# Two fused expert layers behind a causal convolution: some convolutions summed by adding transfers, blocks 0 and 1 interleaved by eight

## The chip, the cores and the metric

The kernel runs on one core of a Trainium2 chip, as one launch. The metric is device time in microseconds. Three runs of the kernel before gave 1137.07, 1137.29 and 1139.7 us; their median, 1137.29 us, is the time to which the change is compared. The engines are named as in the profile: PE multiplies matrices, PEld is its weight load, DVE is VectorE, ACT is ScalarE, POOL is GpSimd, SP only issues transfers.

## The reference, cut to what matters

A causal convolution over 7 tokens, with weights per head made by a softmax, then two layers of "multiply, activate, multiply":

```
w   = softmax(weight)                      # 8 heads x 7 taps; 24 channels share a head
out = sum over k of w[k] * x[t - 6 + k]    # 2 x 4096 tokens, 192 channels
h   = out @ moe_w_in                       # 192 -> 2048
g   = h where h >= 1, 0 where h <= -1, (h + 1)^2 / 4 between
x2  = g @ moe_w_out                        # 2048 -> 192
h2  = x2 @ moe2_w_in
y   = (h2 * sigmoid(1.702 * h2)) @ moe2_w_out
```

Everything is float32 and has to come out with nearly float32's precision.

## The kernel before

**Tiling.** The 8192 tokens are 16 blocks of 512. Channels lie on partitions, tokens along the row. A layer's 2048 hidden channels are 16 groups of 128, numbered f = 0 to 15. One layer of one block is a phase, and one group of one phase is a unit. The 192 channels are two parts: part a is the first 128, part b the last 64; the b parts of two blocks (0 and 1, 2 and 3, and so on) share one tile of 128 partitions.

**Precision.** Each float32 operand is split in two halves of a shorter format, a high one by a copy on ACT (L73 for activations, L127 for weights) and the rest by a subtraction on DVE (L74, and L131 and L132 for weights), and products of halves are added in PSUM.

**A unit.** `gemm1(u)` makes the hidden values of unit u in one of four PSUM banks (5 matmuls, L250). `act_a(u)` activates them: for layer 1 an activation, a square on ACT (L272, L273) and a max-min on DVE (L274). `act_b(u)` splits the result (`ghi` on ACT, `glo` on DVE). `gemm2(u)` adds its product into the block's two output banks (5 matmuls, L315), LAG = 4 steps after `gemm1(u)`. For the first 32 units a step is `gemm1(step)`, `act_a(step)`, `act_b(step - 1)`, `gemm2(step - 4)`, in the lines L493 to L501. From unit 32 on (WHOLE) units go in pairs, with half-size matmuls that run two at a time (`both`, L361).

**Weights.** Weights arrive as 64-bit words and are converted on chip, once for each layer and f, in four pieces (`weight_ops`): `begin` (a Prelu on ACT, L117, tile `wa`, and a shift on DVE, L118, tile `wd`), `join` (DVE, L122), `high_part` (ACT, L127) and `low_part` (DVE, L131 and L132). `gemm1` of a unit needs both parts of its f. Raw words have three buffers, filled by transfers that SP issues.

**Order.** All engines run the program in the order in which the code issues it; no scheduler moves it. `plan` is a table from step to operations, filled by `at(step, op)`; `beside(step)` issues that step's operations. Units 0 to 31 are layer 1 of blocks 0 and 1, interleaved by CH = 4 (`in_turn`, L216): four units of block 0, four of block 1, and so on. Then follow 16 units of block 2, layer 2 of blocks 0 and 1, and layers 1 and 2 of the other blocks.

**Convolutions.** Block 0 and 1's b part and block 1's a part are done on PE, seven float32 matmuls against diagonal matrices (`conv_on_pe`, banks `cb_ps` and `ca_ps`, L170); block 1's diagonals are made by POOL (L167). Block 0's a part, and all of the later blocks, are done on DVE, one multiply and six multiply-adds for a tile (`conv_taps`, L152 and L153). `conv_at(j)` places those of blocks 2j and 2j + 1: for blocks 2 and 3, part a of block 2 in steps 10 to 17, part b of both in steps 18 to 25. `put_a` and `put_b` split the sums into the tiles `xah`, `xal`, `xb`, `xc`, which `gemm1` reads.

Of the kernel before, what the change touches and what calls it, by code (L numbers as in the profile page):

```python
# [8 lines left out]
F32 = mybir.dt.float32  # L9
# [3 lines left out]
ALU = mybir.AluOpType  # L13
# [7 lines left out]
def kernel(  # L21
# [44 lines left out]
    def bank(n, name):  # L66
        return ps.tile([P, T], F32, tag=f"bank{n}", name=name)
# [33 lines left out]
    def weight_ops(n, f, s):  # L101

        low, high = s[:, :, 0], s[:, :, 1]
        w = wt[n][:, f, :]  # L110
# [37 lines left out]
    def conv_taps(part, t, c):  # L148
        def tap(k):
            w, x = taps[:, part, k : k + 1], t[:, k : k + T]  # L150
            if k == 0:
                return lambda: nc.vector.tensor_scalar_mul(c, x, w)  # L152
            return lambda: nc.vector.scalar_tensor_tensor(c, x, w, c, op0=ALU.mult, op1=ALU.add)  # L153

        return [tap(k) for k in range(K)]

    def warm_up():

        w = bank(7, "warm")
        for _ in range(9):  # L160
            nc.tensor.matmul(w[:, 0:P], ident, ident, start=True, stop=True)  # L161

    def conv_on_pe(part, t, c, ident, eng_mul):

        d = o_p.tile([P, K, P], F32, tag="o", name="diag")
        for k in range(K):
            eng_mul(d[:, k], ident, taps[:, part, k : k + 1])  # L167

        def tap(k):
            return lambda: nc.tensor.matmul(c, d[:, k], t[:, k : k + T], start=k == 0, stop=k == K - 1)  # L170

# [9 lines left out]
    def put_b(i, c):  # L181

        b, halved = i % B, phases.index((1, i)) * NF >= WHOLE
        t = x1[i][2 + (b if halved else 0)]
        hi, lo = (t[0:DB], t[DB:P]) if b == 0 else (t[DB:P], t[0:DB])
        split(c[b * DB : (b + 1) * DB], hi, lo)
        if halved:
            swap_halves(x1[i][3 - b], t)

    def conv_ops(j):  # L190

        ta, tb = xt[0, B * j], xt[1, j]
        ca = cv_p.tile([P, T], F32, tag="cva", name="cva")
        cb = cv_p.tile([P, T], F32, tag="cvb", name="cvb", bufs=1)
        x1[B * j] = new_xs()
        ops = conv_taps(0, ta, ca) + [lambda: put_a(B * j, ca)]
        ops += conv_taps(1, tb, cb) + [lambda: put_b(B * j, cb)]
        st = {}

        def begin():  # L200
            st["c"] = cv_p.tile([P, T], F32, tag="cva", name="cva")
            x1[B * j + 1] = new_xs()
            st["ops"] = conv_taps(0, xt[0, B * j + 1], st["c"])
            put_b(B * j + 1, cb)
# [8 lines left out]
        phases += [(1, i), (2, i - 1)]  # L213
    phases += [(2, NBLK - 1)]

    def in_turn(*ps):  # L216
        return [(p, c + f) for c in range(0, NF, CH) for p in ps for f in range(CH)]

    units = in_turn(0, 1) + in_turn(2) + in_turn(3, 4)
    units += [(p, f) for p in range(5, len(phases)) for f in range(NF)]  # L220
    unit_at = {u: k for k, u in enumerate(units)}

# [181 lines left out]
    def at(step, op):  # L404
        plan.setdefault(max(step, 0), []).append(op)
# [14 lines left out]
    def fetch_x(*which):  # L420
        for part, i in which:
            xt[part, i] = x_load(part, i)

    def conv_at(j):
        first, second = (unit_at[phases.index((1, B * j + k)), 0] for k in range(B))
        ops = []
        at(first - 30, lambda: fetch_x((0, B * j), (1, j), (0, B * j + 1)))
        at(first - 22, lambda: ops.extend(conv_ops(j)))
        for k in range(2 * (K + 1)):
            at(first - 22 + k, lambda: ops.pop(0)())  # L430
        for k in range(K + 2):
            at(second - 16 + k, lambda: ops.pop(0)())

    with tc.manual_schedule():
        nc.sync.dma_start(taps, taps_in)
        fetch_x((0, 0), (1, 0))
        fetch_w(1, 0)
        fetch_w(1, 1)
        fetch_x((0, 1))
        fetch_w(1, 2)  # L440

        make_identity(nc, ident)
        warm_up()
        softmax_taps()

        nc.scalar.activation(const.tile([P, 1], F32, name="table"), ident[:, 0:1], AF.Gelu_apprx_sigmoid)
        for i in range(B):
            x1[i] = new_xs()
        ca = cv_p.tile([P, T], F32, tag="cva", name="cva")
        cb_ps, ca_ps = bank(3, "cb_ps"), bank(2, "ca_ps")  # L450
        a0 = conv_taps(0, xt[0, 0], ca)
        b_ops = conv_on_pe(1, xt[1, 0], cb_ps, ident, nc.scalar.mul)
        a1 = conv_on_pe(0, xt[0, 1], ca_ps, ident, nc.gpsimd.tensor_scalar_mul)
        for op in b_ops:
            op()

        ws = [weight_ops(1, f, raw.pop((1, f))) for f in range(CH - 1)]
        order = a0[0:3] + ws[0][0:1] + a0[3:5] + ws[0][1:3] + a0[5:7] + ws[0][3:4] + ws[1][0:1]
        order += [lambda: put_a(0, ca)] + ws[1][1:2] + [lambda: put_b(0, cb_ps)] + ws[1][2:] + ws[2]
        for op in order:  # L460
            op()
        fetch_w(1, 3)
        for k, op in enumerate(weights_at(1, 3)):
            at(k // 2, op)
        for k, op in enumerate(a1):
            at((k + 2) // 3, op)
        at(1, lambda: put_b(1, cb_ps))
        at(2, lambda: put_a(1, ca_ps))

        def convert_at(n, f, steps):  # L470
            at(steps[0] - 3, lambda: fetch_w(n, f))
            for step, op in zip(steps, weights_at(n, f)):
                at(step, op)

        for f in range(CH, NF):
            s = f - 2 if f < 2 * CH else 2 * f - 2 * CH - 1
            convert_at(1, f, range(s, s + 4))
        for f in range(NF):
            s = 2 * NF - 2 + 4 * f if f < CH else 3 * NF - 2 + 2 * (f - CH)
            convert_at(2, f, range(s, s + 4))  # L480
# [99 lines left out]
```

## Time and profile before

| | us |
|---|---|
| median of 3 runs | 1137.29 |
| the profiled execution's own time | 1136.92 |
| its span from first to last instruction | 1135.1 |
| PE busy | 1126.0 |
| ACT busy | 824.1 |
| DVE busy | 715.2 |
| POOL busy | 7.6 |

The span is one execution, and what lies around it is 1136.92 - 1135.1 = 1.82 us. A matmul's end is modelled and matmuls are pipelined, so the distance between the starts of two steps says more on PE than its busy time. The granted TensorE clock is 1.00 of full speed, 2.4 GHz, in every slice of the span. The steps that the change touches lie in the first 93 us: unit 0 starts at 11.58 us and unit 32 at 90.74 us.

### The profile page before, as it was taken

How to read it: one execution, taken by the hardware profiler on the slowest of the kernel's cores; microseconds unless marked ns; L12 is line 12 of the kernel's file. 1: busy time of each engine (PE TensorE's matmuls, PEld its weight loads, DVE VectorE, ACT ScalarE, POOL GpSimd, SP SyncE). 2: the span in 40 equal slices, each digit the busy share in tenths (PEclk: the TensorE clock that was granted, in tenths of full speed). 3: DMA queues.
4: the chain of work that ended last, by engine and by line, in shares of the span. 5: the costliest groups of instructions: out<-in, count | busy, mean ns of one | idle time of the engine just before them, and what ended most of it. 6: DMA issues, size and time to landing. Idle time of an engine off the chain costs nothing.

```text
span 1135.1 us, 23124 instructions
## 1 busy us (share of the span) xinstructions
PE 1126.0 (99%) x9468; PEld 1009.6 (89%) x9468; DVE 715.2 (63%) x1152; ACT 824.1 (73%) x1468; POOL 7.6 (1%) x13
## 2 busy tenths in 40 slices
PE   9999999999999999999999999999999999999998
PEld 5878889999999999999999999999999999999997
DVE  7997866674657756476564756647566575655532
ACT  7988976867758677686876758677586776868654
POOL 2000000000000000000000000000000000000000
PEclk9999999999999999999999999999999999999999
DMA  5312330100001000010000000010000100000000
GB/s 176 125 28 65 111 97 27 57 10 25 11 10 43 18 17 10 11 43 20 15 19 15 30 19 15 20 43 1 20 15 20 43 1 20 15 20 15 11 15 15
DMA packets 16841, 36.69 MB, mean 32 GB/s; under 512 B 2528, under 2 KB 2784, under 8 KB 16736
## 3 DMA queue, kind: packets, MB, share of 16 engines
q1 hardware_dynamic: 16592, 35.09, 10.5%
q8 instruction: 75, 1.23, 0.5%
q14 instruction: 30, 0.25, 0.1%
q10 hardware_dynamic: 144, 0.13, 0.0%
HBM read 21.05 MB, written 6.29 MB: 24 GB/s over the span
## 4 chain that ended last, share of the span: by engine, by line
PE 93%; DVE 3%; ACT 2%; issue 1%; POOL 0%; POOLq 0%; DVEq 0%
PE acc L361 47%; PE h L361 42%; PE acc L315 1%; PE h L250 1%; DVE glo L74 1%; DVE a L274 1%; ACT a L273 1%; ACT a L272 1%; PE cb_ps L170 1%; PE ca_ps L170 1%; DVE wd L122 0%; PE warm L161 0%; ACT ghi L73 0%; ACT wa L117 0%; ACT wt L127 0%
## 5 line engine op out<-in xcount | busy, mean ns | idle before, releaser
L361 PE MATMUL acc<-ghi,wt 64*128 64x512 f32 x2868 | 869.0, 386 | 0.3 <-ACT ghi L73 0.3
L361 PE MATMUL h<-xah,wt 64*128 64x512 f32 x1912 | 738.2, 386 | 0.0
L361 PE MATMUL acc<-glo,wt 64*128 64x512 f32 x1912 | 706.1, 386 | 0.1
L361 PEld LDWEIGHTS acc<-ghi,wt 64*128 64x128 f32 x2868 | 489.6, 184 | 29.8 <-ACT ghi L73 0.7
L74 DVE TENSOR_TENSOR glo<-a,ghi 128x512 fp32r<-128x512 f32 x512 | 341.6, 688 | 228.8 <-ACT ghi L73 218.6
L361 PEld LDWEIGHTS acc<-glo,wt 64*128 64x128 f32 x1912 | 351.8, 184 | 20.1 <-DVE glo L74 0.8
L361 PEld LDWEIGHTS h<-xah,wt 64*128 64x128 f32 x1912 | 351.8, 184 | 19.8 <-issue 0.4
L361 PE MATMUL h<-xal,wt 64*128 64x512 f32 x956 | 369.2, 386 | 0.0
L73 ACT CAST ghi<-a 128x512 fp32r<-128x512 f32 x512 | 301.3, 614 | 28.3 <-DVE a L274 28.1
L274 DVE SCALAR_TENSOR_TENSOR a<-h,a 128x512 f32<-128x512 f32 x256 | 176.9, 691 | 161.3 <-ACT a L273 161.2
L276 ACT ACTIVATE a<-h 128x512 f32<-128x512 f32 x256 | 151.3, 596 | 155.0 <-PE h L361 147.1
L361 PE MATMUL h<-xb,wt 64*128 64x512 f32 x717 | 238.8, 386 | 0.0
L361 PE MATMUL h<-xc,wt 64*128 64x512 f32 x717 | 238.7, 386 | 0.0
L272 ACT ACTIVATE a<-h 128x512 f32<-128x512 f32 x256 | 151.0, 590 | 53.6 <-PE h L361 53.3
L361 PEld LDWEIGHTS h<-xal,wt 64*128 64x128 f32 x956 | 175.9, 184 | 9.7
L273 ACT ACTIVATE a<-a 128x512 f32<-128x512 f32 x256 | 161.8, 632 | 8.2
L361 PEld LDWEIGHTS h<-xc,wt 64*128 64x128 f32 x717 | 131.9, 184 | 9.6
L361 PEld LDWEIGHTS h<-xb,wt 64*128 64x128 f32 x717 | 131.9, 184 | 5.0
L153 DVE SCALAR_TENSOR_TENSOR cva<-xt,taps,cva 128x512 f32<-128x512 f32 x90 | 67.3, 748 | 1.2
L153 DVE SCALAR_TENSOR_TENSOR cvb<-xt,taps,cvb 128x512 f32<-128x512 f32 x42 | 31.3, 746 | 0.4
L250 PE MATMUL h<-xah,wt 128*128 128x512 f32 x68 | 28.3, 417 | 2.6 <-DVE wt L131 2.6
L73 ACT CAST xb<-s 64x512 fp32r<-64x512 f32 x16 | 9.9, 621 | 28.2 <-DVE s L377 28.2
(61 smaller groups left out, 417.8 us busy)
## 6 DMA issues: line engine op xcount, KB each, us to landing
raw<-in_w_dram SPq DMA_DIRECT2D x32, 448.0 KB, 3.5
xc<-xb SPq DMA_DIRECT2D x46, 128.0 KB, 2.2
xt<-in_xa_dram SPq DMA_DIRECT2D x16, 259.0 KB, 3.5
out_dram<-o SPq DMA_DIRECT2D x15, 256.0 KB, 2.0
out_dram<-o SPq DMA_DIRECT2D x17, 128.0 KB, 2.3
xt<-in_xb_dram SPq DMA_DIRECT2D x8, 259.0 KB, 3.2
xb<-xc SPq DMA_DIRECT2D x14, 128.0 KB, 2.2
out_dram<-o ACTq DMA_DIRECT2D x1, 128.0 KB, 1.8
```

Source lines behind the costliest of these rows:

```text
L73: nc.scalar.copy(hi, src)
L74: nc.vector.tensor_sub(lo, src, f32(hi))
L153: return lambda: nc.vector.scalar_tensor_tensor(c, x, w, c, op0=ALU.mult, op1=ALU.add)
L170: return lambda: nc.tensor.matmul(c, d[:, k], t[:, k : k + T], start=k == 0, stop=k == K - 1)
L250: nc.tensor.matmul(h, w, r, start=j == 0, stop=j == len(prods) - 1)
L272: nc.scalar.activation(a, h, AF.Relu, bias=0.5, scale=0.5)
L273: nc.scalar.activation(a, a, AF.Square)
L274: nc.vector.scalar_tensor_tensor(a, h, 1.0, a, op0=ALU.max, op1=ALU.min)
L276: nc.scalar.activation(a, h, AF.Gelu_apprx_sigmoid)
L315: nc.tensor.matmul(acc, w, r, start=id(acc) in fresh, stop=last and ends[id(acc)] == k)
L361: mm = nc.tensor.matmul(banks[n], w, r, start=n in fresh, stop=ends.get(n) == k)
```

## The change

- Block 1's part a, block 2's part a and the b part shared by blocks 2 and 3 are convolved by `conv_by_dma`: the first tap is a multiplication into the sum `c`, and each of the other six is a multiplication into a scratch tile `y` and a transfer, issued by POOL, that adds `y` to `c`. For block 1 all seven multiplications are on ACT; for blocks 2 and 3 the even taps are on DVE and the odd ones on ACT. Before, block 1's part a was on PE, the other two on DVE.
- Blocks 0 and 1 take turns by 8 units, not by 4.
- Layer 1's conversions come earlier: those of f = 0 to 4 begin ahead of step 0, those of f = 5 to 15 are in steps f - 5 to f - 2 (f up to 7) and 2f - 12 to 2f - 9.
- In steps 0 to 7 the step's planned operations come before the activation, not after `gemm2`.
- Block 2's taps are in steps 9 to 21 (odd) with `put_a` in 24, the b part's in 10 to 22 (even) with `put_b` in 25.

```diff
+    def conv_by_dma(part, t, c, muls, scratch):
+        def tap(k):
+            w, x, mul = taps[:, part, k : k + 1], t[:, k : k + T], muls[k % len(muls)]
+            def op():
+                if k == 0:
+                    mul(c, x, w)
+                else:
+                    y = scratch()
+                    mul(y, x, w)
+                    nc.gpsimd.dma_start(c, y, accum_op=ALU.add)
+            return op
+        return [tap(k) for k in range(K)]
...
-        ops = conv_taps(0, ta, ca) + [lambda: put_a(B * j, ca)]
-        ops += conv_taps(1, tb, cb) + [lambda: put_b(B * j, cb)]
+        if j == 1:
+            muls = nc.vector.tensor_scalar_mul, nc.scalar.mul
+            def scratch():
+                return o_p.tile([P, T], F32, tag="o", name="y")
+            ops = conv_by_dma(0, ta, ca, muls, scratch) + [lambda: put_a(B * j, ca)]
+            ops += conv_by_dma(1, tb, cb, muls, scratch) + [lambda: put_b(B * j, cb)]
+        else:
...
-    units = in_turn(0, 1) + in_turn(2) + in_turn(3, 4)
+    units = in_turn(2 * CH, 0, 1) + in_turn(CH, 2) + in_turn(CH, 3, 4)
...
+        if j == 1:
+            steps = [*range(9, 9 + 2 * K, 2), 24, *range(10, 10 + 2 * K, 2), 25]
+            at(2, lambda: fetch_x((0, B * j), (1, j)))
+            at(12, lambda: fetch_x((0, B * j + 1)))
...
-        a1 = conv_on_pe(0, xt[0, 1], ca_ps, ident, nc.gpsimd.tensor_scalar_mul)
+        a1 = conv_by_dma(0, xt[0, 1], ca1, (nc.scalar.mul,), lambda: f32(g_p.tile([P, T], F32R, tag="glo", name="y")))
...
-        order = a0[0:3] + ws[0][0:1] + a0[3:5] + ws[0][1:3] + a0[5:7] + ws[0][3:4] + ws[1][0:1]
-        order += [lambda: put_a(0, ca)] + ws[1][1:2] + [lambda: put_b(0, cb_ps)] + ws[1][2:] + ws[2]
+        order = a0[0:3] + ws[0][0:1] + more[0:1] + a0[3:5] + ws[0][1:3] + a1[0:2] + a0[5:7] + ws[0][3:4] + ws[1][0:1] + more[1:2] + a1[2:3]
+        order += [lambda: put_a(0, ca)] + ws[1][1:2] + [lambda: put_b(0, cb_ps)] + ws[1][2:3] + ws[2][0:1] + more[2:3]
+        order += ws[1][3:] + ws[2][1:3] + ws[3][0:1] + more[3:4] + ws[3][1:2] + ws[4][0:1] + more[4:5]
...
+        for f, done in ((2, 3), (3, 2), (4, 1)):
+            for k, op in enumerate(ws[f][done:]):
+                at(k, op)
+        for k, op in enumerate(a1[3:]):
             at(k // 2, op)
...
+        at(3, lambda: put_b(1, cb_ps))
+        at(6, lambda: put_a(1, ca1))
...
-            s = f - 2 if f < 2 * CH else 2 * f - 2 * CH - 1
+        for f in range(CH + 1, NF):
+            s = f - 5 if f < 2 * CH else 2 * f - 3 * CH
...
             gemm1(step)
+            if step < 2 * CH:
+                beside(step)
             act_a(step)
...
+            if step >= 2 * CH:
+                beside(step)
```

On PE, between the b convolution and unit 4, the program before has (h0 to h4 are the hidden banks of units 0 to 4; the diagonal of `ca_ps` is block 1's part a):

```order
L170 MATMUL cb_ps_139<-xt_95,diag_141 128x512 x7
L250 MATMUL h0_201<-xah_130,wt1_88 128x512
...
L170 MATMUL ca_ps_140<-xt_101,diag_149 128x512
L250 MATMUL h1_221<-xah_130,wt1_88 128x512
...
L170 MATMUL ca_ps_140<-xt_101,diag_149 128x512 x3
L250 MATMUL h2_245<-xah_130,wt1_88 128x512
...
L170 MATMUL ca_ps_140<-xt_101,diag_149 128x512 x3
L250 MATMUL h3_276<-xah_130,wt1_88 128x512
```

and the changed program has at the same place:

```order
L186 MATMUL cb_ps_139<-xt_95,diag_141 128x512 x7
L275 MATMUL h0_215<-xah_130,wt1_88 128x512
...
L275 MATMUL h1_239<-xah_130,wt1_88 128x512
...
L275 MATMUL h2_269<-xah_130,wt1_88 128x512
...
L275 MATMUL h3_295<-xah_130,wt1_88 128x512
```

The seven matmuls of `ca_ps` are gone, and nothing stands between the first units.

On ACT, from the first weight's `high_part` to the first activation, the program before has:

```order
L127 CAST wt1_88<-wd_168 128x448
L117 ACTIVATE wa_179<-raw_99 128x448
L73 CAST xah_130<-cva_138 128x512
L73 CAST xb_132<-cb_ps_139 64x512
L127 CAST wt1_88<-wd_180 128x448
L117 ACTIVATE wa_191<-raw_103 128x448
L127 CAST wt1_88<-wd_192 128x448
L272 ACTIVATE a_207<-h0_201 128x512
```

and the changed program has, from the third weight's `high_part` to the second activation's neighbours (the rows ahead of these are `high_part`, first tap, one `y`, `begin`, one more `y`, the two copies of block 0, `high_part` and `begin`):

```order
L127 CAST wt1_88<-wd_193 128x448
L117 ACTIVATE wa_202<-raw_163 128x448
L117 ACTIVATE wa_209<-raw_181 128x448
L127 CAST wt1_88<-wd_203 128x448
L166 ACTIVATE y_225<-xt_101,taps_85 128x512
L166 ACTIVATE y_228<-xt_101,taps_85 128x512
L117 ACTIVATE wa_231<-raw_196 128x448
L297 ACTIVATE a_235<-h0_215 128x512
L298 ACTIVATE a_235<-a_235 128x512
L127 CAST wt1_88<-wd_210 128x448
L166 ACTIVATE y_248<-xt_101,taps_85 128x512
L166 ACTIVATE y_251<-xt_101,taps_85 128x512
```

Four more conversions' begins or high parts, the first tap and four products `y` now stand ahead of the first activation.

On DVE, around the last conversion of layer 1 (f = 15), the changed program has (a_771 is unit 21's activation, glo_776 unit 20's split):

```order
L122 SCALAR_TENSOR_TENSOR wd_711<-wa_710,wd_711 128x448
L299 SCALAR_TENSOR_TENSOR a_748<-h20_742,a_748 128x512
L74 TENSOR_TENSOR glo_753<-a_723,ghi_752 128x512
L299 SCALAR_TENSOR_TENSOR a_771<-h21_765,a_771 128x512
L74 TENSOR_TENSOR glo_776<-a_748,ghi_775 128x512
L131 TENSOR_TENSOR wt1_88<-wd_711,wt1_88 128x384
L132 TENSOR_TENSOR wt1_88<-wd_711,wt1_88 128x64
```

The last `low_part` stands behind unit 21's activation, and its reader is `gemm1` of unit 23; before, it stood behind unit 24's, and its reader was unit 27.

## Rows read from the trace of the kernel before

**Rows 1.** The page's line of busy time, share and instructions.
```profile
PE 1126.0 (99%) x9468; PEld 1009.6 (89%) x9468; DVE 715.2 (63%) x1152; ACT 824.1 (73%) x1468; POOL 7.6 (1%) x13
```
**Rows 2.** Stretches: us, busy time of PE, PEld, DVE, ACT, POOL, granted clock, DMA share, GB/s.
```profile
40.00:60.00 20.00, 18.97 (x84) 15.42 (x83) 19.21 (x39) 17.43 (x33) 0.00 (x0) 1.00 0.30 93
60.00:80.00 20.00, 18.40 (x81) 14.73 (x80) 19.95 (x40) 17.13 (x32) 0.00 (x0) 1.00 0.00 0
```
**Rows 3.** Chain that ended last, to 60 us: start, us, what.
```profile
14.26 0.86 PE ca_ps L170 x2
...
16.28 2.58 PE ca_ps L170 x6
...
20.00 2.58 PE ca_ps L170 x6
```
**Rows 4.** Waits to 100 us: engine, line, releaser, total us, times, longest.
```profile
ACT wt L127 <- DVE wd L122: 7.2, 10, 1.5
...
PE h L250 <- DVE wt L131: 2.6, 2, 1.6
```
**Rows 5.** Timeline of PE: start, us, instruction, idle before it: units 5, 6, 27, 28.
```profile
26.15 0.39 PE L250 MATMUL h<-xah,wt 128*128 128x512 f32 x1
...
28.42 0.39 PE L250 MATMUL h<-xah,wt 128*128 128x512 f32 x1
...
79.26 0.50 PE L250 MATMUL h<-xah,wt 128*128 128x512 f32 x1 [1.60 <-DVE wt L131]
...
81.67 0.39 PE L250 MATMUL h<-xah,wt 128*128 128x512 f32 x1
```
**Rows 6.** Timeline of ACT: the start, and one step with a conversion.
```profile
8.74 0.56 ACT L127 CAST wt<-wd 128x448 fp32r<-128x448 f32 x1 [1.48 <-DVE wd L122]
...
12.18 0.58 ACT L73 CAST xb<-cb_ps 64x512 fp32r<-64x512 f32 x1 [1.34 <-PE cb_ps L170]
...
30.26 0.56 ACT L127 CAST wt<-wd 128x448 fp32r<-128x448 f32 x1
30.73 0.62 ACT L117 ACTIVATE wa<-raw 128x448 f32<-128x448 f32 x1
31.25 0.57 ACT L272 ACTIVATE a<-h 128x512 f32<-128x512 f32 x1
31.86 0.63 ACT L273 ACTIVATE a<-a 128x512 f32<-128x512 f32 x1
32.39 0.60 ACT L73 CAST ghi<-a 128x512 fp32r<-128x512 f32 x1
32.90 0.56 ACT L127 CAST wt<-wd 128x448 fp32r<-128x448 f32 x1
```
**Rows 7.** Timeline of DVE: shift, activation, split, low part, join.
```profile
66.45 0.39 DVE L118 TENSOR_SCALAR wd<-raw 128x448 uint32<-128x448 uint32 x1
...
67.41 0.69 DVE L274 SCALAR_TENSOR_TENSOR a<-h,a 128x512 f32<-128x512 f32 x1
68.02 0.69 DVE L74 TENSOR_TENSOR glo<-a,ghi 128x512 fp32r<-128x512 f32 x1
68.61 0.55 DVE L131 TENSOR_TENSOR wt<-wd,wt 128x384 fp32r<-128x384 f32 x1
...
69.22 0.62 DVE L122 SCALAR_TENSOR_TENSOR wd<-wa,wd 128x448 uint32<-128x448 uint32 x1
```
**Rows 8.** DMA issues of the page, and landings of `xt` to 60 us.
```profile
xc<-xb SPq DMA_DIRECT2D x46, 128.0 KB, 2.2
...
out_dram<-o SPq DMA_DIRECT2D x15, 256.0 KB, 2.0
...
DMA to landing us min/median/max: 3.0/5.2/5.7
```
**Rows 9.** Timelines of DVE and POOL: a shift beside POOL's multiplications.
```profile
10.81 0.48 DVE L118 TENSOR_SCALAR wd<-raw 128x448 uint32<-128x448 uint32 x1
...
4.17 6.88 POOL L167 TENSOR_SCALAR diag<-ident,taps 128x128 f32<-128x128 f32 x7 [2.89 <-DVE taps L90]
```

More of the change, by code (lines that the diff above doesn't have):

```diff
@@ L195, in conv_ops @@
         x1[B * j] = new_xs()
-        ops = conv_taps(0, ta, ca) + [lambda: put_a(B * j, ca)]
-        ops += conv_taps(1, tb, cb) + [lambda: put_b(B * j, cb)]
+        if j == 1:
[5 more added lines that the diff above has]
+        else:
+            ops = conv_taps(0, ta, ca) + [lambda: put_a(B * j, ca)]
+            ops += conv_taps(1, tb, cb) + [lambda: put_b(B * j, cb)]
         st = {}
@@ L214, with in_turn @@
     phases += [(2, NBLK - 1)]
-    def in_turn(*ps):
-        return [(p, c + f) for c in range(0, NF, CH) for p in ps for f in range(CH)]
-    units = in_turn(0, 1) + in_turn(2) + in_turn(3, 4)
+    def in_turn(ch, *ps):
+        return [(p, c + f) for c in range(0, NF, ch) for p in ps for f in range(ch)]
+    units = in_turn(2 * CH, 0, 1) + in_turn(CH, 2) + in_turn(CH, 3, 4)
     units += [(p, f) for p in range(5, len(phases)) for f in range(NF)]
@@ L426, in conv_at @@
         ops = []
[L427 to L430, printed above, removed]
+        if j == 1:
+            steps = [*range(9, 9 + 2 * K, 2), 24, *range(10, 10 + 2 * K, 2), 25]
+            at(2, lambda: fetch_x((0, B * j), (1, j)))
+            at(12, lambda: fetch_x((0, B * j + 1)))
+        else:
+            steps = range(first - 22, first - 22 + 2 * (K + 1))
+            at(first - 30, lambda: fetch_x((0, B * j), (1, j), (0, B * j + 1)))
+        at(steps[0], lambda: ops.extend(conv_ops(j)))
+        for k, step in enumerate(steps):
+            at(step, lambda k=k: ops[k]())
         for k in range(K + 2):
-            at(second - 16 + k, lambda: ops.pop(0)())
+            at(second - 16 + k, lambda k=k: ops[2 * (K + 1) + k]())
     with tc.manual_schedule():
@@ L449 @@
         ca = cv_p.tile([P, T], F32, tag="cva", name="cva")
-        cb_ps, ca_ps = bank(3, "cb_ps"), bank(2, "ca_ps")
+        cb_ps = bank(3, "cb_ps")
+        ca1 = cv_p.tile([P, T], F32, tag="cva", name="cva")
         a0 = conv_taps(0, xt[0, 0], ca)
         b_ops = conv_on_pe(1, xt[1, 0], cb_ps, ident, nc.scalar.mul)
-        a1 = conv_on_pe(0, xt[0, 1], ca_ps, ident, nc.gpsimd.tensor_scalar_mul)
+        a1 = conv_by_dma(0, xt[0, 1], ca1, (nc.scalar.mul,), lambda: f32(g_p.tile([P, T], F32R, tag="glo", name="y")))
         for op in b_ops:
             op()
-        ws = [weight_ops(1, f, raw.pop((1, f))) for f in range(CH - 1)]
-        order = a0[0:3] + ws[0][0:1] + a0[3:5] + ws[0][1:3] + a0[5:7] + ws[0][3:4] + ws[1][0:1]
-        order += [lambda: put_a(0, ca)] + ws[1][1:2] + [lambda: put_b(0, cb_ps)] + ws[1][2:] + ws[2]
+        ws = [weights_at(1, f) for f in range(CH + 1)]
+        more = [lambda f=f: fetch_w(1, f) for f in range(CH - 1, 2 * CH)]
+        order = a0[0:3] + ws[0][0:1] + more[0:1] + a0[3:5] + ws[0][1:3] + a1[0:2] + a0[5:7] + ws[0][3:4] + ws[1][0:1] + more[1:2] + a1[2:3]
+        order += [lambda: put_a(0, ca)] + ws[1][1:2] + [lambda: put_b(0, cb_ps)] + ws[1][2:3] + ws[2][0:1] + more[2:3]
+        order += ws[1][3:] + ws[2][1:3] + ws[3][0:1] + more[3:4] + ws[3][1:2] + ws[4][0:1] + more[4:5]
         for op in order:
             op()
-        fetch_w(1, 3)
-        for k, op in enumerate(weights_at(1, 3)):
+        for f, done in ((2, 3), (3, 2), (4, 1)):
+            for k, op in enumerate(ws[f][done:]):
+                at(k, op)
+        for k, op in enumerate(a1[3:]):
             at(k // 2, op)
[L465 to L468, printed above, removed]
+        at(3, lambda: put_b(1, cb_ps))
+        at(6, lambda: put_a(1, ca1))
         def convert_at(n, f, steps):
-            at(steps[0] - 3, lambda: fetch_w(n, f))
+            if (n, f) not in raw:
+                at(steps[0] - 3, lambda: fetch_w(n, f))
             for step, op in zip(steps, weights_at(n, f)):
                 at(step, op)
-        for f in range(CH, NF):
-            s = f - 2 if f < 2 * CH else 2 * f - 2 * CH - 1
+        for f in range(CH + 1, NF):
+            s = f - 5 if f < 2 * CH else 2 * f - 3 * CH
             convert_at(1, f, range(s, s + 4))
@@ L500 @@
             finish_if_last(step - LAG - 1, step)
-            beside(step)
+            if step >= 2 * CH:
+                beside(step)
         act_b(WHOLE - 1)
```

## The prediction

> **What bounds the kernel now.** I read the page's busy line first: PE is busy for 99% of the span, ACT for 73%, DVE for 63% [rows 1]. So nothing that leaves PE's work alone can be worth more than PE's idle time, 1135.1 - 1126.0 = 9.1 us, and the question is where PE loses time or does work that could go. The stretches come second: from 40 to 80 us DVE is busy 19.21 and then 19.95 of 20 us, and PE only 18.97 and 18.40 [rows 2]. In every stretch from 200 to 1000 us PE is full, and there the change alters nothing. Third, the chain of waits over the first 60 us: it goes through the seven float32 matmuls of `ca_ps`, 0.86 + 2.58 + 2.58 = 6.02 us [rows 3]. Fourth, the waits: twice PE stands for a weight's low part, together 2.6 us [rows 4]. The second is unit 27, for f = 15; it costs more than the 1.60 us shown, since the matmuls around it are stretched and unit 28 starts 2.41 us behind unit 27 where an undisturbed step takes 28.42 - 26.15 = 2.27 us [rows 5].
>
> So the first 32 units end where the slowest of three queues lets them: PE at 2.27 us a step, DVE with the conversions and taps, ACT with conversions and activations. Unit 28 starts at 81.67 us [rows 5]; from there both programs do the same, apart from the convolution of block 2, which is then done in either. The whole difference is when unit 28 starts in the changed program.
>
> **What the change takes away.** PE loses `ca_ps`: 6.02 us. DVE loses 14 taps for blocks 2 and 3 and gets 8 plain multiplications, and does the last conversion three steps earlier. If PE alone decided, 6.02 us and the waits for weights would go.
>
> **What it adds to ACT.** I price ACT by the distance between starts in a stretch where it never waits [rows 6]: high part 0.47, begin 0.52 (30.73 to 31.25; 0.51 elsewhere), activation 0.61, square 0.53, split 0.51. A step without conversion is 1.65 us, with a whole one 2.64 us. That is above PE's 2.27. Before, whole conversions in successive steps stop after f = 7, units of four make room, and afterwards it is half a conversion a step: 2.15 us. Now f = 5 to 7 stand one a step behind five more begun ahead of step 0, and ACT has 13 products more: seven for block 1, six for blocks 2 and 3. Their price is not in the trace. The nearest row is the square, 512 columns from SBUF, 0.53; bounds from the same rows are 0.47 (the shorter cast) and 0.63 (the square's whole duration, as if each waited for the last). I take 0.53.
>
> **Walk along ACT.** Start: the first high part at 8.74 [rows 6] is unchanged. Behind it now stand first tap, `y`, begin, `y`: 8.74 + 0.47 + 0.53 + 0.53 + 0.51 + 0.53 = 11.31 us for block 0's `xah`, which DVE needs for `xal` before it may do the next join. Then ACT and DVE take turns, each waiting for the other's last result: `xb` at 12.18 (unchanged, PE's sum [rows 6]), `xal` until 12.6, join until 13.2, high part and begin until 14.2; on DVE `xb`, shift, low part and join until 15.2; high part and two begins until 16.8; join until 17.0. So the fourth high part starts at 17.0 us, and from there ACT has all its inputs.
>
> From 17.0 to the activation of unit 9: 7 high parts (3.3), 4 products (2.1), 6 begins (3.1), 9 activations with squares (10.3), 8 splits (4.1) and two copies for block 1 (1.0) are 23.9 us: 40.9 us. On the way unit 0's activation starts at 19.1, unit 1's at 22.3, unit 2's at 24.9, unit 3's at 27.5 and unit 4's at 30.2. DVE puts the low part of f = 4 behind unit 1's activation and split, and so on to f = 7 behind unit 4's: 30.2 + 1.24 (ACT's two) + 0.61 + 0.59 + 0.55 [rows 7] = 33.2 us. There unit 7 starts on PE, and unit 8 at 33.2 + 2.27 = 35.5 us; before it was 26.15 + 3 x 2.27 = 32.96. So the 6.02 us are spent already: PE waits for weights where it did the taps, and 2.6 us more.
>
> From unit 9 to unit 21's activation ACT has 12 steps of 1.65 (19.8), 6 high parts (2.8), 5 begins (2.6) and 6 products (3.2): 28.4 us, or 2.37 a step against PE's 2.27. In three of the steps (10, 14, 18: no product ahead of the high part) ACT is at the high part before DVE has joined it: behind the activation's start DVE needs 0.61 + 0.63 for ACT, then activation 0.61, split 0.59, low part 0.61 and join 0.62 [rows 7], 3.7 us, where ACT needs two steps, 3.3: three waits of 0.4, of the kind of which the trace has ten with 7.2 us [rows 4]. So unit 21's activation starts at 40.9 + 28.4 + 1.2 = 70.5 us.
>
> The last low part, f = 15, is behind it on DVE: activation and square 1.25, DVE's activation 0.61, split 0.59, low part 0.55 [rows 7]: 73.6 us. Unit 23 reads it. PE would be there at 35.5 + 15 x 2.27 = 69.6, so it waits 4 us, part of it one unit earlier for f = 14. Then nothing holds PE: 2.41 for the first step behind a wait, four of 2.27 [rows 5], and unit 28 starts at 85.1 us.
>
> **What hides elsewhere.** DVE has 2 x 1.2 + 0.39 + 0.61 + 0.62 and one multiplication a pair of steps, about 4.4 us against ACT's 4.9, so it only waits for ACT; its bound of before is gone, and ACT is late next. The raw words keep three buffers and arrive before their begins, some 3.4 us after issue against 5 us for three begins. The diagonals that leave POOL were beside PE's work and gain nothing.
>
> **The adding transfers.** No row shows one. From below: a plain transfer of the same 256 KB lands after 2.0 us, one of 128 KB between tiles after 2.2 [rows 8]. From above: the slowest landing of an `xt` tile beside the weights, 5.7 us [rows 8]. An adding transfer reads two operands, so I take 3.5, a little over midway to the slow end of the plain ones. POOL issues them in turn, each waiting for the last on the same sum. Block 1's third product is ready at 18.1, so the sixth transfer lands at 18.1 + 4 x 3.5 = 32.1; ACT copies the sum at 33.5. Behind that copy stand a high part and unit 6's activation. The margin holds up to 3.85 us each; above that each 0.1 us costs 0.4, and at 5.7 us the first, whose product is ready at 10.4, sets the pace: the sixth lands at 10.4 + 6 x 5.7 = 44.6, 11.1 us late. For blocks 2 and 3 the spacing is two steps, 4.7 us or more.
>
> The Trainium skill (DMA: Bandwidth & Descriptors, Anatomy of one DMA, the SWDGE path) gives for transfers that POOL issues about 2.0 us plus the bytes over 436 GB/s, an estimate of 2.6 us here. By it the transfers are hidden and the sum stays; no run here shows one.
>
> POOL beside DVE is shown: a shift takes 0.48 us while POOL multiplies, and 0.39 without [rows 9, 7]. The Trainium skill (SBUF — State Buffer, Who interferes with whom) goes further: a DVE operation in a two-port mode locks GpSimd out for its whole duration, and with it the writing of a transfer's descriptors. By that rule each transfer could wait for a shift or multiplication. From the row, 0.39 us on 3.5 makes 3.9, the sixth lands 0.2 us late, and the time is 0.2 us more.
>
> **Sum.** Unit 28 at 85.1 instead of 81.7: +3.5 us. In parts: -6.0 (taps of `ca_ps`), +8.6 (waits for the first weights, making unit 8 2.6 us later), +4.2 (waits for f = 14 and 15 and the stretched step), -3.3 (the waits of before from unit 8 on, 81.67 - 32.96 - 20 x 2.27). The profiled execution took 1136.92 us, which makes 1140.4; the median of the runs is 0.37 above it, so I predict 1140.8 us.
>
> **Bounds.** The products at 0.47 or 0.63 give 13 x -0.06 or +0.10: -0.8 to +1.3. The start's turns may be 1 us off either way, and the three join waits may vanish: without them +2.3. So this case alone runs from 1138 to 1143.
>
> **Rivals.**
> - *PE decides, and the change is faster.* The 6.02 us go, and with the waits for weights 3.3 more: 1137.3 - 9.3 = 1128; with half of ACT's excess hidden, 1133. For it: PE at 99%, and four steps of LAG between activation and use. Against it: ACT's 52 us of work from 17.0 on stand ahead of the last weight, and no LAG applies to a weight. Chance 0.12, with all that ends under 1133.9.
> - *Half of it.* ACT's products cost less or run beside its waits, and the last low part comes near PE's 69.6: within a few us of 1137. Chance 0.15.
> - *The adding transfers are the bound, slower.* At 4.5 us each the sixth lands at 10.4 + 6 x 4.5 = 37.4 and block 1's copy, with all of ACT behind it, is 3.9 us late: 1144.7. It decides from 3.85 us each on. For it: two operands to read, weights in the same engines up to 30 us. Against it: 2.0 and 2.2 us for plain transfers. Chance 0.23.
> - *The change moves PE's clock.* The longest wait of PE in these steps is 1.60 us at a granted clock of 1.00 [rows 5, 2]; I foresee some of 2.1 to 2.7 between units 1 and 4. If it fell to 1.2 GHz, a step would be up to 4.5 us instead of 2.6; two such steps give +4: 1145. Chance 0.05.
>
> **Chances and range.** My case has 0.45. About 0.3% (3.4 us) is what a measurement can tell from no change, so faster means under 1133.9 and slower over 1140.7. My case lies on that line: half of its chance is slower. Faster 0.12; same 0.15 + 0.23 = 0.38; slower 0.22 + 0.23 + 0.05 = 0.50. The range, with a tenth left out on each side, is 1134.5 to 1147; my own case's is 1138 to 1143.
>
> **What would show it.** Right: PE idle before units 2, 3 and 4 for 2 us or more each, released by DVE's low part; ACT without idle time from 17 to 70 us; the largest PE wait at unit 23; unit 28 near 85 us; the sixth adding transfer landed before 33 us. Wrong: unit 8 before 33 us, or PE without a wait at unit 23 (then PE decides); ACT waiting at block 1's `xah` for a transfer, or for a scratch tile (then the transfers do); a clock below 1.00.

## The result, and the profile after

| | median us (lowest to highest) | ratio to before, 95% interval |
|---|---|---|
| before | 1137.18 (1136.95 to 1139.7), 4 runs | |
| after | 1152.3 (1150.67 to 1152.89), 4 runs | 1.0131 [1.0118, 1.0144] |

The change made the kernel slower by 15.1 us. The prediction was 1140.8 us with a range of 1134.5 to 1147: the direction was right, the size was not. The profiled execution of the changed kernel has a span of 1150.6 us against 1135.1 us.

The page's busy line answers to [rows 1]. PE has 14 matmul records fewer, and is busy for 2.3 us longer.

```profile
PE 1128.3 (98%) x9454; PEld 1009.8 (88%) x9454; DVE 710.3 (62%) x1146; ACT 832.2 (72%) x1481; POOL 16.5 (1%) x24
```

The stretches answer to [rows 2], with four short ones added.

```profile
40.00:60.00 20.00, 20.00 (x90) 16.57 (x89) 16.70 (x35) 18.53 (x35) 1.58 (x2) 1.00 0.41 124
60.00:80.00 20.00, 17.56 (x69) 12.81 (x68) 15.90 (x33) 16.75 (x32) 6.18 (x8) 0.95 0.57 111
16.00:20.00 4.00, 2.00 (x8) 1.02 (x6) 2.46 (x7) 3.81 (x8) 0.99 (x1) 1.00 0.76 217
24.00:28.00 4.00, 0.82 (x2) 0.10 (x1) 0.69 (x1) 3.34 (x7) 0.86 (x1) 0.50 0.63 146
80.00:84.00 4.00, 2.32 (x7) 1.47 (x6) 2.53 (x5) 3.94 (x8) 0.86 (x1) 0.81 0.56 102
84.00:88.00 4.00, 3.43 (x9) 2.74 (x10) 2.65 (x7) 2.07 (x5) 1.73 (x2) 0.62 0.51 94
```

DVE is no longer full from 40 to 80 us, as forecast. But PE does 0.82 us of work from 24 to 28 us, and its granted clock is 0.50 there, that is 1.2 GHz. From 60 to 80 us the transfer engines, which moved nothing before, are busy for 0.57 of the time. From 20 to 24 us they are full, and were at 0.18 before (the changed kernel's stretch first, then that of before): the adding transfers are in these steps, and the loads of `xt` for blocks 2 and 3 now start at 20.28 us instead of 24.68.

```profile
20.00:24.00 4.00, 1.65 (x4) 1.39 (x5) 2.13 (x5) 2.06 (x4) 0.00 (x0) 0.51 1.02 331
20.00:24.00 4.00, 3.99 (x14) 1.94 (x12) 3.32 (x7) 3.28 (x7) 0.00 (x0) 1.00 0.18 73
```

Where PE waits stands in its timeline, which answers to [rows 5]. The rows are the starts of units 2, 3, 4, 5, 6, 8, 22, 23 and 28.

```profile
18.37 0.50 PE L275 MATMUL h<-xah,wt 128*128 128x512 f32 x1 [1.79 <-DVE wt L131]
22.35 0.77 PE L275 MATMUL h<-xah,wt 128*128 128x512 f32 x1 [2.56 <-DVE wt L132]
30.60 0.79 PE L275 MATMUL h<-xah,wt 128*128 128x512 f32 x1 [5.78 <-DVE wt L131]
35.16 0.49 PE L275 MATMUL h<-xah,wt 128*128 128x512 f32 x1 [0.54 <-DVE wt L131]
38.07 0.50 PE L275 MATMUL h<-xah,wt 128*128 128x512 f32 x1 [0.33 <-DVE wt L131]
...
42.72 0.39 PE L275 MATMUL h<-xah,wt 128*128 128x512 f32 x1
...
78.22 0.80 PE L275 MATMUL h<-xah,wt 128*128 128x512 f32 x1 [1.72 <-DVE wt L131]
84.57 0.50 PE L275 MATMUL h<-xah,wt 128*128 128x512 f32 x1 [2.25 <-DVE wt L131]
...
97.64 0.39 PE L275 MATMUL h<-xah,wt 128*128 128x512 f32 x1
```

Each wait in brackets is put down to DVE's low part, so one has to ask what DVE waited for. The chain of waits says it; only its transfers and what leads from them to unit 4 are shown (start, us, what).

```profile
16.95 7.66 DMA cva<-y
24.61 0.03 issue
24.65 0.49 issue
25.14 4.16 DMA cva<-y
29.29 0.03 issue
29.34 0.04 issue
29.39 0.17 DVE glo L74
29.55 0.44 issue
30.00 0.55 DVE wt L131
...
37.26 3.83 DMA cva<-y
41.11 0.62 ACT xah L73
```

Block 1's second adding transfer lands 7.66 us after its issue. The third adds to the same sum and is issued only then; it lands after 4.16 us more. Its scratch tile has the tag `glo`, so it holds a buffer of the ordinary splits: DVE's split at 29.39 us waits for that landing, the low part of f = 4 stands behind it on DVE, and unit 4 on PE behind that. DVE's timeline shows this wait for a buffer, with its releaser, and a later one for the fifth transfer, ahead of the low part that unit 6 reads.

```profile
29.39 0.69 DVE L74 TENSOR_TENSOR glo<-a,ghi 128x512 fp32r<-128x512 f32 x1 [1.68 <-DMA cva<-y]
...
36.86 0.69 DVE L74 TENSOR_TENSOR glo<-a,ghi 128x512 fp32r<-128x512 f32 x1 [0.35 <-DMA cva<-y]
```

ACT's timeline shows another, of a product for a scratch tile that the second transfer still reads.

```profile
24.63 0.72 ACT L166 ACTIVATE y<-xt,taps 128x512 f32<-128x512 f32 x1 [2.54 <-DMA cva<-y]
```

The issues on POOL's timeline give the pace of block 1's six transfers: 10.93, 16.95, 25.14, 29.82, 33.58 and 37.26 us. The view of `cva` over each issue gives their landings: 5.5, 7.7, 4.2, 3.2, 3.2 and 3.8 us. Each issue starts some 0.5 us behind the landing before it (0.03 and 0.49 us of "issue" in the chain above). The six landings, 27.6 us, and five such gaps are the whole way from 10.93 us to the sixth landing at 37.26 + 3.83 = 41.09. Block 1's copy on ACT follows at 41.11 us, and from there ACT does not wait until unit 9's activation at 48.60 us.

```profile
10.93 1.01 POOL L167 DMA_DIRECT2D cva<-y  x1 [9.63 <-ACT y L166]
16.95 0.99 POOL L167 DMA_DIRECT2D cva<-y  x1 [5.00 <-ACT wa L117]
25.14 0.86 POOL L167 DMA_DIRECT2D cva<-y  x1 [7.20 <-DMA cva<-y]
```

The view of the tile `cva` has all twelve landings on it, of block 1 and block 2.

```profile
DMA to landing us min/median/max: 3.2/3.2/7.7
```

### The profile page after: what moved, and what is told of

It is laid out like the page before. It is cut to its first block, busy times and chain, and to the rows that moved or that the text cites. A ratio compares the mean times of both kernels' runs of the same rounds, so it can differ in the third digit from the quotient of the medians.

```text
span 1150.6 us, 23166 instructions
## 1 busy us (share of the span) xinstructions
PE 1128.3 (98%) x9454; PEld 1009.8 (88%) x9454; DVE 710.3 (62%) x1146; ACT 832.2 (72%) x1481; POOL 16.5 (1%) x24
## 3 DMA queue, kind: packets, MB, share of 16 engines
q1 hardware_dynamic: 16592, 35.09, 10.4%
## 4 chain that ended last, share of the span: by engine, by line
PE 92%; DMA 3%; ACT 2%; DVE 1%; issue 1%; SPq 0%; POOL 0%; POOLq 0%; DVEq 0%; ACTq 0%
PE acc L386 47%; PE h L386 42%; DMA cva<-y 2%; PE acc L340 2%; PE h L275 1%; ACT a L297 0%; ACT a L298 0%; ACT wt L127 0%; DMA raw<-in_w_dram 0%; DVE wd L122 0%; ACT y L166 0%; ACT wa L117 0%; DVE glo L74 0%; ACT ghi L73 0%; DVE wt L131 0%
## 5 line engine op out<-in xcount | busy, mean ns | idle before, releaser
L153 DVE SCALAR_TENSOR_TENSOR cva<-xt,taps,cva 128x512 f32<-128x512 f32 x84 | 62.8, 747 | 1.2
L275 PE MATMUL h<-xah,wt 128*128 128x512 f32 x68 | 29.3, 431 | 15.3 <-DVE wt L131 12.6
L275 PEld LDWEIGHTS h<-xah,wt 128*128 128x128 f32 x68 | 13.6, 200 | 22.5 <-DVE wt L131 16.1
L340 PE MATMUL acc<-ghi,wt 128*128 128x512 f32 x102 | 30.8, 410 | 0.6 <-ACT ghi L73 0.6
```

Source lines behind the costliest of these rows:

```text
L275: nc.tensor.matmul(h, w, r, start=j == 0, stop=j == len(prods) - 1)
L340: nc.tensor.matmul(acc, w, r, start=id(acc) in fresh, stop=last and ends[id(acc)] == k)
```

## The experiments

Theory: the adding transfers set the pace of the start, since each waits for the last on one sum and shares the transfer engines with the weights. Rivals (other explanations): the new order and ACT's load alone, the addition by itself, and PE's clock. The table has every kernel; us against before is the ratio's distance from 1 times 1137 us, and the unit columns are starts on PE in the profiled execution.

| kernel | median us | ratio, interval | us against before | unit 8 | unit 23 | unit 28 |
|---|---|---|---|---|---|---|
| before | 1137.18 | | | 32.95 | 68.27 | 81.67 |
| after | 1152.3 | 1.0131 [1.0118, 1.0144] | +14.9 | 42.72 | 84.57 | 97.64 |
| a1_on_pe | 1143.6 | 1.0053 [1.0034, 1.0072] | +6.0 | 34.32 | 75.53 | 88.33 |
| b23_on_dve | 1148.66 | 1.0103 [1.0088, 1.0119] | +11.7 | 44.57 | 83.38 | 96.45 |
| order_only | 1139.05 | 1.002 [1.0011, 1.003] | +2.3 | 34.32 | 72.64 | 84.15 |
| before_b23_dma | 1138.56 | 1.0013 [1.0003, 1.0022] | +1.5 | 33.98 | 70.85 | 84.26 |
| unchained | 1144.34 | 1.0059 [1.0044, 1.0073] | +6.7 | 38.62 | 76.04 | 89.12 |
| plain_transfers | 1146.49 | 1.0086 [1.0072, 1.01] | +9.8 | 40.50 | 78.47 | 91.52 |
| extra_loads | 1157.45 | 1.0181 [1.0165, 1.0198] | +20.6 | 42.20 | 89.17 | 102.29 |
| fill_pe | 1152.56 | 1.0137 [1.0122, 1.0151] | +15.6 | 45.21 | 86.39 | 97.89 |
| taps_later | 1135.95 | 0.9989 [0.998, 0.9998] | -1.3 | 32.76 | 67.22 | 80.60 |
| taps_later_w | 1135.03 | 0.9983 [0.9974, 0.9992] | -1.9 | 33.33 | 67.33 | 79.42 |

**Parts of the change.** Four kernels undo or do one part.

a1_on_pe, the changed kernel with block 1's part a back on PE (main line of the edit; the calls' places move with it):

```diff
...
-        a1 = conv_by_dma(0, xt[0, 1], ca1, (nc.scalar.mul,), ...)
+        a1 = conv_on_pe(0, xt[0, 1], ca_ps, ident, nc.gpsimd.tensor_scalar_mul)
```

> The changed kernel with block 1's part a back on PE against diagonals; blocks 2 and 3 keep the transfers, the order by 8 stays. Theory (the adding transfers of block 1, chained beside the weight loads, are what failed): ACT loses 7 products of 0.62 us and both kinds of waits for transfers; unit 8 starts near 33 us and unit 23 near 74 us instead of 84.6; 1141.5 us (1139.5 to 1143.5). Rival (the order by 8 with conversions first is itself the cost): unit 4 still starts after 28 us, 1149 us or more.

b23_on_dve, the changed kernel with the taps of blocks 2 and 3 done as before (the same edit stands once more in `conv_at`, for their steps):

```diff
-        if j == 1:
+        if j == 0:
             muls = nc.vector.tensor_scalar_mul, nc.scalar.mul
```

> The changed kernel with the convolutions of blocks 2 and 3 back on DVE as taps in steps 10 to 25; block 1 keeps its transfers. Theory (these transfers cost about 3 us: 2.4 us of ACT's waits and 0.5 of dear products, but DVE's 14 taps of 0.66 us come back at 2.66 us a step against ACT's 2.74 now): 1151 us (1149.5 to 1152.5). Rival (they are the main cost): 1145 us or less.

order_only, both of these edits, so that no adding transfer is left:

> The changed kernel without any transfer that adds: block 1's part a on PE, blocks 2 and 3 on DVE; what stays is the order by 8, conversions first, and the plan ahead of the activation in steps 0 to 7. Theory: unit 9's activation near 38 us, then DVE bounds at 2.66 us a step, unit 23 near 73 us, 1140.5 us (1138.5 to 1143). Rival (the order alone costs nothing, all loss is in the transfers): 1137 us or less.

before_b23_dma, the kernel before with `conv_by_dma` for blocks 2 and 3 alone (cut; the steps 9 to 25 come with it):

```diff
...
-        ops = conv_taps(0, ta, ca) + [lambda: put_a(B * j, ca)]
+            ops = conv_by_dma(0, ta, ca, muls, scratch) + [lambda: put_a(B * j, ca)]
```

> The kernel before, in its own order, with only the convolutions of blocks 2 and 3 done by products and adding transfers in steps 9 to 25. Theory (it trades DVE's waits of 3.3 us for ACT's 6 products and waits for scratch tiles): 1137 us (1135 to 1139.5). Rival (transfers that land in 3.2 us are free here): DVE no longer makes PE wait and the time is 1134 us.

order_only and before_b23_dma came out within the theory's bounds. a1_on_pe (1143.6) is 0.1 us above its bounds and b23_on_dve (1148.66) 0.8 below; from the rivals' bounds they are 5.4 and 3.7 us away. The order costs 2.3 us, the transfers of blocks 2 and 3 on top of it 6.0 - 2.3 = 3.7 (3.2 with block 1's beside them: 14.9 - 11.7), and block 1's 14.9 - 6.0 = 8.9 (9.4 without the others: 11.7 - 2.3). So block 1's six transfers, with their products on ACT, are more than half of the loss. With them undone, unit 8 starts at 34.32 us: the new order without the transfers is 1.2 us better there than I had forecast for the whole change (35.5).

**The chain.** unchained gives each of the 18 transfers a scratch tile and, in turn, one of six destinations of its own (cut; shown is the transfer):

```diff
...
-                    nc.gpsimd.dma_start(c, y, accum_op=ALU.add)
+                    nc.gpsimd.dma_start(own(), y, accum_op=ALU.add)
```

> The changed kernel in which each transfer adds into a tile of its own (cleared ahead by POOL) and takes its product from a scratch tile of its own, so that none waits for another and nothing waits for a scratch tile; the convolutions' sums are thus left out, only the first tap reaches the blocks. Number and size of the transfers and all products stay. Theory (the waits for transfers make the loss beyond the forecast walk along ACT): unit 8 near 35.5 us, unit 23 near 74 to 75, 1142 us (1140 to 1144.5). Rival (ACT's products and the weights' late arrival beside transfers are the loss, the chain is not): 1148 us or more.

The time fell inside the theory's bounds, near their upper end; units 8 and 23, at 38.62 and 76.04 us, came 3.1 and 1.0 us later than the theory had them. 14.9 - 6.7 = 8.2 us go with the chain, though single transfers take as long as before or longer. The tile `spares` holds scratch and destinations:

```profile
DMA to landing us min/median/max: 3.2/3.5/8.6
```

So a slow landing costs nothing while nobody waits for it. With no transfer to wait for, ACT never waits for more than 0.3 us from 18.5 to 77 us. Unit 9's activation starts 1.8 us behind the 40.9 that the prediction gave it:

```profile
42.70 0.58 ACT L313 ACTIVATE a<-h 128x512 f32<-128x512 f32 x1
```

Unit 21's starts 30.3 us later, at 72.96 (29.6 in the prediction), and unit 23 on PE 3.08 us behind that. PE's clock is at half in the first steps here too:

```profile
24.00:28.00 4.00, 2.59 (x7) 1.58 (x6) 3.11 (x7) 3.94 (x8) 0.85 (x1) 0.50 1.07 280
28.00:32.00 4.00, 4.00 (x11) 3.03 (x11) 3.94 (x8) 3.90 (x8) 0.00 (x0) 0.50 1.07 296
```

From 28 to 32 us PE is busy throughout and does 11 matmuls, where at full clock it does 19 or 20 in four us. ACT does not wait for PE there, so this costs nothing further on; behind unit 23 the half clock does cost: units 23 to 28 take 13.08 us instead of the 11.5 forecast. This experiment takes away two waits at once, for the sum and for the shared buffers of `glo`; how the 8.2 us divide between them stays open. The trace of the changed kernel speaks against scratch of its own as a remedy by itself: the landings and their gaps alone put block 1's copy at 41.1 us. That was not run.

**The addition.** plain_transfers keeps tiles, queue and order, and copies instead of adding:

```diff
-                    nc.gpsimd.dma_start(c, y, accum_op=ALU.add)
+                    nc.gpsimd.dma_start(c, y)
```

> The changed kernel with its 18 transfers made plain: the same tiles, queue and order, each still waiting for the last on the same sum, but the bytes overwrite the sum instead of being added to it, so the convolutions of these parts are left out of the result. Theory: what makes the first transfers of block 1 land 6.0 and 7.7 us after their issue is the weight loads in flight beside them, and the addition has only the smaller part of it: alone a transfer lands in 2.0 to 2.6 us instead of 3.2, but the first two still take 5 us or more each, unit 8 starts at 40 to 42.5 us, and the time is 1149 to 1152 us. Rival: the addition itself is the cost: no transfer takes over 4 us, unit 8 starts at 39 us or earlier, and the time is 1147 us or less.

This came out between the two. The time (1146.49) is the rival's, unit 8 (40.50) and the slowest landing are the theory's, and the first two transfers, at 4.3 and 4.4 us, are below the theory's 5. The view of `cva` has the landings:

```profile
DMA to landing us min/median/max: 2.2/2.4/6.1
```

The slowest is block 1's third, in the chain of waits:

```profile
21.01 6.08 DMA cva<-y
```

And this is one issue on POOL's timeline, away from the weights:

```profile
51.88 0.54 POOL L167 DMA_DIRECT2D cva<-y  x1 [17.60 <-DVE glo L74]
```

A plain transfer beside the weights still takes up to 6.1 us instead of 2.4, so the crowd does not need the addition. The addition makes a transfer 0.8 us longer when it is alone (3.2 against 2.4; POOL's own part 0.86 against 0.54) and costs 14.9 - 9.8 = 5.1 us in all; block 1's six plain transfers take 25.3 us from the first issue to the last landing, the adding ones 30.2.

**The crowd.** extra_loads adds 13 loads of 448 KB, as large as a weight's and into a tile that nothing reads, in steps 10 to 22, where the transfers of blocks 2 and 3 run:

```diff
+        for f in range(3, NF):
+            at(f + 7, lambda f=f: nc.sync.dma_start(spares[:, f, :], words[2][f].bitcast(U32)))
```

> The changed kernel with one plain load of 448 KB more in each of the steps 10 to 22, into memory that nothing uses until layer 2's weights are made there. Theory (an adding transfer takes 4 to 8 us instead of 3.2 when weight loads share the engines): the transfers of blocks 2 and 3, 3.2 us now, become 5 to 7 us, ACT waits for scratch tiles about 2 us more at each product, 1160 us (1156 to 1166). Rival (the first transfers were long because they were POOL's first, or for DVE's port): they stay at 3.2 us and the time at 1152 to 1153.5.

The theory held in the time and in the transfers beside the loads, not in all of them: of the twelve for blocks 2 and 3 the five issued from 55.17 to 71.22 us landed after 6.3 to 7.8 us, the seven behind them after 3.2 to 3.8. Unit 8 starts 0.5 us earlier than in the changed kernel, unit 23 4.6 us later. The view of the scratch tile `y` has all 18 landings, and ACT's waits for such a tile to 100 us have one of 5.7 us (total, times, longest):

```profile
DMA to landing us min/median/max: 3.2/3.7/7.8
ACT y L167 <- DMA cva<-y: 6.9, 2, 5.7
```

**The clock.** fill_pe puts idle matmuls (7, 10, 24, 9 and 9) ahead of units 2, 3, 4, 22 and 23:

```diff
+        for _ in range({2: 7, 3: 10, 4: 24, 22: 9, 23: 9}.get(u, 0)):
+            nc.tensor.matmul(h, hidden_w(u - 1)[0][:, 0:P], ah, start=True, stop=True)
```

> The changed kernel with idle matmuls in PE's gaps ahead of units 2, 3, 4, 22 and 23 (7, 10, 24, 9 and 9, of 0.23 us each at full clock, into the bank that the unit then clears). Theory (the clock that falls to half in these gaps costs only behind unit 23, where PE is late: units 23 and 24 take 1.7 us more than at full clock): the granted clock stays 1.00 from 20 to 100 us, 1150.5 us (1149.5 to 1151.5). Rival (the clock costs more, since units 3 to 8 are also late by it): 1147 us or less. Rival (nothing): 1152.3.

The time did not move, against my expectation. The clock did:

```profile
24.00:28.00 4.00, 4.00 (x19) 3.30 (x19) 0.69 (x1) 3.49 (x7) 0.86 (x1) 1.00 0.88 246
```

Units 4, 5 and 6 still start at 30.93, 35.48 and 38.39 us, no earlier than in the changed kernel (30.60, 35.16, 38.07): up to there the weights set the pace, and a faster PE only waits longer. From unit 23 to 28 it takes 11.50 us instead of 13.07, so there the half clock costs 1.6 us. This was lost again earlier, when unit 7 came 2.4 us later behind a split on DVE that waits for a scratch tile:

```profile
41.60 0.69 DVE L74 TENSOR_TENSOR glo<-a,ghi 128x512 fp32r<-128x512 f32 x1 [2.23 <-DMA cva<-y]
```

In the changed kernel the same split starts at 38.97 us and does not wait for that transfer. So the idle matmuls moved more than the clock, and what the clock costs in the whole time is not shown, only that it costs nothing up to unit 6 and 1.6 us behind unit 23.

**A better version of before.** The waits that the change was to remove can be reached without transfers. taps_later moves the taps of blocks 2 and 3 four steps later; taps_later_w also begins the conversions of f = 8 to 15 one step earlier:

```diff
-            at(first - 22 + k, lambda: ops.pop(0)())
+            at(first - (18 if j == 1 else 22) + k, lambda: ops.pop(0)())
-            s = f - 2 if f < 2 * CH else 2 * f - 2 * CH - 1
+            s = f - 2 if f < 2 * CH else 2 * f - 2 * CH - 2
```

> The kernel before with one edit: the taps of blocks 2 and 3 in steps 14 to 29 instead of 10 to 25. Theory (before unit 28 DVE bounds the kernel before, and the waits for the low parts of f = 11 and f = 15 stand behind taps): four taps of 0.66 us fewer ahead of either, both waits go, 1134 us (1133.3 to 1135). Rival (the taps' work comes back as a late xb for unit 32): 1137 to 1138.

> The kernel before with the taps of blocks 2 and 3 in steps 14 to 29 and layer 1's conversions of f = 8 to 15 one step earlier (steps 2f - 10 to 2f - 7). Theory: on VectorE the order alone sets the wait: the low part of f = 15 then stands one step of 2.27 us further ahead of unit 27, so the 1.6 us wait there goes, unit 28 starts at 79.0 to 79.6 us instead of 80.6 (kernel with the taps alone later) and 81.7 (before), and the time is 1134 to 1135 us. Rival: the conversions only take the place of activations and splits on VectorE, and the wait comes back at another unit: unit 28 at 80.5 us or later, and 1136 us or more.

taps_later gained 1.3 us (0.9 between the medians), and its time lies between the theory's bounds and the rival's: the wait before unit 19 fell from 1.03 us to 0.17, unit 27's did not change. The first row is of the kernel before, the others of taps_later.

```profile
59.07 0.50 PE L250 MATMUL h<-xah,wt 128*128 128x512 f32 x1 [1.03 <-DVE wt L131]
58.02 0.50 PE L250 MATMUL h<-xah,wt 128*128 128x512 f32 x1 [0.17 <-DVE wt L131]
...
78.20 0.50 PE L250 MATMUL h<-xah,wt 128*128 128x512 f32 x1 [1.60 <-DVE wt L131]
```

taps_later_w removes that one too: units 27 and 28 start without a wait.

```profile
77.16 0.39 PE L250 MATMUL h<-xah,wt 128*128 128x512 f32 x1
...
79.42 0.39 PE L250 MATMUL h<-xah,wt 128*128 128x512 f32 x1
```

At 1135.03 us (11 runs, 1134.08 to 1135.67) it is the fastest kernel here, 1.9 us or 0.17% below the kernel before; the time is 0.03 us above the theory's bounds, unit 28 inside them, and the interval excludes 1.

## Why the prediction was wrong in size

- **The failing step** is the price of an adding transfer, "so I take 3.5", which has the sixth landing at 32.1 us. A transfer alone lands in 3.2 us, but block 1's first three ran beside the loads and took 5.5, 7.7 and 4.2. The 0.5 us between a landing and the next issue the prediction put at nothing, so that even undisturbed transfers on one sum stand 3.7 us apart. The sixth landed at 41.09 us, which is 5.03 us for each, and "block 1's copy" on ACT, put at 33.5, came at 41.11, 7.6 late.
- **How it was chosen.** 3.5 is not "a little over midway": the middle between 2.0 and 5.7 is 3.85, just the margin that the prediction names. The bound from above was better: that `xt` load of 5.7 us was issued at 3.05 us, beside the first weights, and those issued from 24.68 to 25.63 us took 5.1 to 5.5 [rows 8]. The prediction chose by the nearest kind of transfer, not by the nearest stretch.
- **A near hit that is luck.** At 5.7 us the prediction has the sixth transfer 11.1 us late, which is 1140.8 + 11.1 = 1151.9 us; measured was 1152.3. But the copy was only 7.6 us late, and the rest came from the terms below. The rival "the adding transfers are the bound" named the mechanism. At the measured 5.03 us its rule gives 10.4 + 6 x 5.03 - 33.5 = 7.1 us, or 1147.9; I priced it at 4.5 us each, 1144.7, which set the end of the range too low as well.
- **Waits that I had not priced.** The prediction watched for ACT to wait for the sum or for a scratch tile. Both occurred (0.89 and 2.54 us), but the largest wait of PE, 5.78 us ahead of unit 4, goes through DVE's split, which shares its buffers with the scratch. The scratch tiles of blocks 2 and 3 stood in the sum with nothing. They have two buffers, so a product waits for the landing of the transfer two before it, though these land in the ordinary 3.2 us:

```profile
66.53 0.73 ACT L166 ACTIVATE y<-xt,taps 128x512 f32<-128x512 f32 x1 [1.17 <-DMA cva<-y]
...
78.11 0.72 ACT L166 ACTIVATE y<-xt,taps 128x512 f32<-128x512 f32 x1 [1.23 <-DMA cva<-y]
```

- **ACT's walk.** Up to the fourth high part it was 0.6 us off (17.58 against 17.0). Unit 9's activation was put at 40.9 and started at 48.60, +7.7. From there to unit 21's activation I gave 29.6 us; it took 81.49 - 48.60 = 32.89, +3.3: mostly the two waits for scratch tiles, 1.17 and 1.23 us, and products that cost more than the 0.53 taken. The three short waits for joins came nearly as forecast, 0.32, 0.32 and 0.31 us against 0.4. A product lasts 0.717 us and the next instruction follows 0.62 behind it, just under my upper bound of 0.63. The price could have been had: the Trainium skill (ScalarE: Activation LUTs, What ACT_TABLE_LOAD costs) gives an activation 186 ns, 0.833 ns a column and 93 ns for each per-partition operand, an estimate of 0.71 us here, and the trace agrees.
- **The tail.** From unit 21's activation to unit 23 I gave 3.1 us (its terms add up to 3.0); it took 84.57 - 81.49 = 3.08. PE waits there for the last low parts, as forecast, with 1.72 and 2.25 us.
- **PE's clock** was a rival at 0.05. It fell to 0.50 at the start and again near 79 and 85 us. Up to unit 6 it cost the changed kernel nothing (fill_pe); units 23 to 28 took 13.07 us instead of the 11.5 forecast, +1.6.
- **The sum.** 7.7 + 3.3 + 1.6 = 12.6 us, and unit 28 came at 97.64 instead of 85.1, 12.5 late. The time is 11.5 above the forecast: behind unit 28 the profiled execution needs 0.3 us less than before, and it lies 0.3 us above the median, where that of before lay 0.4 below.
- **Right:** PE waits ahead of units 2, 3 and 4 (1.79, 2.56 and 5.78 us, where 2 or more was forecast for each); DVE's bound of before is gone; nothing of the 6.02 us on PE was gained. The walk along ACT held where no transfer is waited for: 30.3 us from unit 9's to unit 21's activation in unchained, against 29.6. That order_only has unit 28 at 84.15 us, near my 85.1 for the whole change, is luck: it has none of the 13 products on ACT, and DVE is its full engine, with 19.18 of 20 us from 60 to 80.
- **Transfers by the page.** The Trainium skill's estimate of 2.6 us (DMA: Bandwidth & Descriptors, Anatomy of one DMA) is near the 2.4 measured for a plain transfer alone and below the 3.2 of an adding one. The same page's section "Issuing engines are not separate DMA queues" says that transfers of all issuing engines run on the same 16 engines and interleave; the 6.1 us of a plain one beside SP's weight loads agrees with it, and I had not used it. The rule of the Trainium skill in SBUF — State Buffer (Who interferes with whom), that DVE can lock POOL out, left no clear mark: POOL's issues of `cva` last 0.86 to 1.01 us, and one at 22.86 us in extra_loads, beside a shift on DVE, lasts 0.86.

## What to carry to other kernels

Price a transfer by the stretch in which it runs, not by its kind: here the slowest landing of a neighbour, 5.7 us, was nearer to what the first transfers took (5.5, 7.7 and 4.2) than the price of one alone. A chain of transfers on one sum costs the sum of its landings and a gap between each two, and whatever shares a buffer with its scratch waits along. Without the chain the same transfers cost 8.2 us less; starting it when no loads are in flight, or giving it scratch of its own, was not tried. When work leaves a busy engine, ask first which waits can be removed by moving it a few steps on the same engine; here that gave the only gain.

## What the runs showed of the hardware

- An adding transfer of 256 KB between tiles, issued by POOL, takes 3.2 us alone, a plain one 2.4; POOL is held for 0.86 and 0.54 us. Beside 448 KB loads the same take up to 7.8 us (extra_loads; 7.7 in the changed kernel) and 6.1.
- When each transfer adds to the same sum, the next issue starts some 0.5 us behind a landing (from 24.61 to 25.14 us in the changed kernel).
- In unchained the granted clock was 0.50, or 1.2 GHz, from 16 to 32 us, though PE's waits up to 16 us were no longer than 1.27 us (before unit 0) and PE was busy for 2.35 of the four us ahead of 16. In the changed kernel it fell at about 20 us, with no wait of PE's up to then above 1.79. The prediction looked for a long pause as the cause.
- Idle matmuls kept the clock at 1.00 and gained nothing where a weight was awaited (units 4 to 6 in fill_pe).
